# More weight tiles converted ahead of the second batch's folds, and more products behind those folds

## The chip, the cores and the metric

The kernel runs on one core of a Trainium2 chip. The metric is the device time of one execution in microseconds (us). The tensor engine is PE, its weight loads PEld, the vector engine DVE, the scalar engine ACT, GpSimd POOL, and SyncE, which here only issues transfers, SP. "L650" is line 650 of the kernel's file.

## The reference, cut to what matters

```python
# 4 batches, 8 heads, 768 rows, 64 wide; blocks of 64 rows: attention with decay
out[:, :, sl] = intra + inter                    # -> x of (4, 768, 512)
mixed = np.real(fft(fft(x, axis=1), axis=2))     # mix over rows, then over columns
u  = x + mixed
un = (u - mean(u)) / sqrt(var(u) + 1e-6)
ch = maximum(un @ w_ch1, 0) @ w_ch2              # 512x2048 and 2048x512, given as f64
return u + ch
```

## The kernel before: the parts that matter

A front (attention, folds of the rows, spectral products, norm) makes the rows of one batch after another. Beside it run the products with the weights of four groups of rows, the plain tiles (L636 with w1, L650 with w2); they fill PE while a front waits for DVE. The other eight groups, the late tiles, come last, as pairs with fewer products, and need linear combinations of the weights and of their own operands.

The weights arrive as f64 words and are converted on DVE and ACT, 32 tiles by one generator `w`. The front's generator yields a weight after each step, and the schedule puts so many units of products behind that step:

```python
            run(fold_a(b))
            yield 6.0 if b - 1 in LEADS else 3.0      # LEADS = (0,), so b = 1 here
            run(fold_b(b, sets))
            yield 12.0 if b - 1 in LEADS else 9.0     # L508
```

```python
    run(beside(mix, 24.0, beside(att1, 2.75 * t_chunk, w, 0.16 * NW), 0.16 * NW + 1.75 * t_chunk))
    half = [[mlp(b, g, h * FO // 2, (h + 1) * FO // 2) for b, g in PLAIN[:3]] for h in range(2)]
    ...
    t_rest, t_back = 3 * t_front - 5 * t_chunk, len(PLAIN) * t_mlp - 50.0   # 50.0: kept for the end
    ...
    run(weave(fr, back, (t_back - t_half) / (t_rest - t_rest * t_half / t_back)))
    front_end.close()
    ...
    load_u(0, nc.scalar)
    run(weave(combine_weights(0), back, 1.5))
    run(back)
    plain_end.close()
    psums.close()
    ...                                      # pools of the late tiles; p2: accumulators, 8 banks
    run(combine_weights(1))
    for j in range(len(LATE) // 2):
        late(j)
```

The boundary between the plain and the late tiles: what DVE does there.

```python
    def combine_weights(part):               # 16 pieces of 128x1024 on DVE, at L700
        if part == 0:
            todo = [(ws[:, 0], a21, a22, ADD), ...  # 3 sums of w1 -> w1s, 6 pieces
                    (wz[:, 0], b12, b11, SUB), ...] # 3 sums of w2 -> w2s, 6 pieces
        else:
            todo = [(a21, a11, a21, SUB), (b12, b22, b12, SUB)]   # in place, 4 pieces
        for o, x, y, op in todo:
            ...
                V.tensor_tensor(o[:, i:i + n // 2], x[:, i:i + n // 2], y[:, i:i + n // 2], op=op)
                yield 1.3

    # end of a plain tile (mlp), L660 to L663: ps is the accumulator of L650
                y = new(up, [128, DM], "y", bufs=1)
                tt(y[:, 0:HM], ps[:, 0:HM], u[:, 0:HM], op=ALU.add)                    # L661
                tt(y[:, HM:DM], ps[:, HM:DM], u[:, DM - 1:HM - 1:-1], op=ALU.add)      # L662
                store(b, T, y)               # L623: nc.sync.dma_start(...)

    def late(j):
        V.tensor_tensor(t[:, 0], b12, b11, op=SUB)       # L713 to L716: combinations "us"
        ...
            X, Y, Z = bank(), bank(), bank()
            prod(X, "a11", "b11", i, True)               # L723, needs no combination
            prod(Y, "a12", "b21", i, True)               # L723, needs none either
            prod(X, "s2", "t2", i, False)                # L723, needs w1s and us
```

## Time and profile before

| | before |
|---|---|
| time, median of 3 (range) | 823.18 us (821.59 to 825.39) |
| profiled span | 819.4 us |
| start to the first product with w1 | 96.2 us |
| first product with w1 to the first late product (L723): "the middle" | 331.9 us, PE idle 6.5 |
| first late product to the last addition on DVE (L799): "the late stage" | 388.2 us, PE idle 0.5 |

The last three rows are read off the lists of instructions in order of time; the 3.1 us by which their sum falls short of the span lie behind the last addition, where its result is stored. The profile's own lines are in the prediction below.

### The profile page before, as it was taken

To read this page: it belongs to the slowest core of one execution; us is meant where nothing else is said; L and a number is where in the kernel's file an instruction comes from. 1 tells how busy PE (TensorE), PEld (TensorE's weight loads), DVE (VectorE), ACT (ScalarE), POOL (GpSimd) and SP (SyncE) were. 2 spreads that over 40 slices of the span, in tenths; PEclk is the share of its full clock that TensorE was granted. 3 is DMA by queue.
4 is the path that set the end of the run, shared out by engine and by line. 5 is a ranking of instruction groups with operands and counts; after the bars stand their busy time and mean duration, and the time that the engine had idled before them with its cause. 6 is when DMAs were issued, how large, how long until landed. Compare 5 with 4: busy or idle time off the path is not lost.

```text
span 819.4 us, 11694 instructions
## 1 busy us (share of the span) xinstructions
PE 795.2 (97%) x4608; PEld 634.9 (77%) x4608; DVE 437.8 (53%) x1018; ACT 186.5 (23%) x448; POOL 86.1 (11%) x102
## 2 busy tenths in 40 slices
PE   6989899999999999999999999999999999999998
PEld 5777767768585857768648888888888888888886
DVE  5899798766743761354895541165313661146311
ACT  3756344225420211312002200022001210022100
POOL 3223340011011010220000000000000000000000
PEclk9999999999999999999999999999999999999999
DMA  9979624248741136530351011100111001010010
GB/s 233 249 154 271 174 90 129 63 113 201 203 125 51 52 62 131 129 123 26 93 162 42 1 53 51 52 1 1 64 40 52 0 1 39 33 33 0 1 39 26
DMA packets 126684, 68.88 MB, mean 84 GB/s; under 512 B 111150, under 2 KB 112174, under 8 KB 126630
## 3 DMA queue, kind: packets, MB, share of 16 engines
q1 hardware_dynamic: 121488, 55.67, 26.6%
q0 software_dynamic: 2112, 6.69, 2.4%
q10 hardware_dynamic: 3030, 5.78, 1.9%
q8 instruction: 36, 0.59, 0.3%
q14 instruction: 18, 0.15, 0.1%
HBM read 48.72 MB, written 19.40 MB: 83 GB/s over the span
## 4 chain that ended last, share of the span: by engine, by line
PE 80%; DVE 10%; issue 4%; DMA 3%; ACT 2%; POOL 1%; POOLq 0%; ACTq 0%; DVEq 0%
PE p L770 24%; PE p L723 24%; PE pm L650 10%; PE pm L636 8%; PE pa L332 3%; PE pa L516 3%; PE pa L298 3%; DMA x<-xb,ix 2%; PE pa L328 2%; PE pa L274 1%; DVE sc L302 1%; PE pa L315 1%; PE pa L348 1%; PE pa L279 1%; DVE stt L546 1%
## 5 line engine op out<-in xcount | busy, mean ns | idle before, releaser
L636 PE MATMUL pm<-ut,w 128*128 128x256 f32 x512 | 119.2, 382 | 0.0
L650 PE MATMUL pm<-w,hr 128*128 128x512 f32 x256 | 115.8, 597 | 0.2 <-DVE w L225 0.2
L636 PEld LDWEIGHTS pm<-ut,w 128*128 128x128 f32 x512 | 94.4, 190 | 15.4 <-issue 3.6
L723 PE MATMUL p<-ur,w 128*128 128x256 f32 x384 | 93.8, 379 | 0.0
L650 PEld LDWEIGHTS pm<-w,hr 128*128 128x128 f32 x256 | 46.6, 190 | 49.5 <-issue 48.0
L723 PEld LDWEIGHTS p<-ur,w 128*128 128x128 f32 x384 | 73.0, 190 | 10.3 <-issue 0.5
L723 PE MATMUL p<-us,w1s 128*128 128x256 f32 x256 | 65.7, 379 | 0.0
L770 PE MATMUL p<-w,hs 128*128 128x256 f32 x256 | 58.0, 379 | 0.5 <-DVE y L791 0.5
L770 PE MATMUL p<-w2s,hs 128*128 128x256 f32 x256 | 57.9, 379 | 0.0
L770 PE MATMUL p<-w,ha 128*128 128x256 f32 x256 | 57.9, 379 | 0.0
L770 PEld LDWEIGHTS p<-w,hs 128*128 128x128 f32 x256 | 48.5, 190 | 7.5 <-DVE y L791 0.9
L625 POOL DMA_INDIRECT out_dram<-y,ix x12 | 11.9, 989 | 402.6 <-DVE y L796 342.6
L770 PEld LDWEIGHTS p<-w2s,hs 128*128 128x128 f32 x256 | 48.6, 190 | 6.6
L723 PEld LDWEIGHTS p<-us,w1s 128*128 128x128 f32 x256 | 48.6, 190 | 6.6
L770 PEld LDWEIGHTS p<-w,ha 128*128 128x128 f32 x256 | 48.6, 190 | 6.6
L750 ACT COPY ha<-p 128x256 f32<-128x256 f32 x32 | 11.9, 372 | 169.1 <-PE p L723 139.4
L761 DVE TENSOR_TENSOR ha<-p,ha 128x256 f32<-128x256 f32 x32 | 13.6, 424 | 45.2 <-ACT ha L760 45.2
L298 PEld LDWEIGHTS pa<-qT,kT 64*128 64x128 f32 x384 | 26.0, 193 | 13.2 <-ACT qT L281 7.3
L302 DVE TENSOR_TENSOR sc<-pa,decay 128x512 f32<-128x512 f32 x48 | 31.5, 683 | 8.8 <-PE pa L298 8.5
L332 PE MATMUL pa<-sc,v 128*64 128x128 f32 x384 | 32.1, 284 | 4.1 <-DVE sc L302 4.1
L298 PE MATMUL pa<-qT,kT 64*128 64x128 f32 x384 | 30.7, 292 | 3.2 <-ACT qT L281 2.9
L270 POOL TENSOR_TENSOR kd<-k,decay 128x512 f32<-128x512 f32 x20 | 23.0, 1152 | 94.8 <-PE pa L315 64.5
(144 smaller groups left out, 1135.0 us busy)
## 6 DMA issues: line engine op xcount, KB each, us to landing
raw<-in_moe_w_ch_dram SPq DMA_DIRECT2D x32, 512.0 KB, 4.8
k<-in_k_dram SPq DMA_DIRECT2D x24, 256.0 KB, 5.0
q<-in_q_dram SPq DMA_DIRECT2D x24, 256.0 KB, 5.9
v<-in_v_dram SPq DMA_DIRECT2D x24, 256.0 KB, 4.9
ud<-x SPq DMA_DIRECT2D x16, 256.0 KB, 2.3
utd<-e SPq DMA_DIRECT2D x64, 64.0 KB, 2.2
u<-ud SPq DMA_DIRECT2D x16, 256.0 KB, 2.7
ur<-utd SPq DMA_DIRECT2D x6, 512.0 KB, 4.3
```

What stands on the lines that cost most here:

```text
L270: nc.gpsimd.tensor_tensor(kd, kt, kpow, op=ALU.mult)
L298: mm(pss[hi][:, hp, :], lhsT=kT[HD[hi], hp, :], rhs=qT[HD[hi], hp, :], start=True, stop=True)
L302: nc.vector.tensor_tensor(t, pss[hi], decay[:, hi::2, :], op=ALU.mult)
L328: mm(po[HD[hi], hp, :], lhsT=s_old[HD[hi], hp, :], rhs=qs[HD[hi], hp, :], start=(hp == 0), stop=False, skip_group_check=True)
L332: mm(po[HD[hi], hp, :], lhsT=vt[:, 2 * hp + hi, :], rhs=sc[hi][:, hp, :], start=(c == 0 and hp == 0), stop=(hp == HP - 1), skip_group_chec ...
L516: mm = nc.tensor.matmul(ps[0:m, n, :], lhsT=piece(a, i, n), rhs=cs[0:rows, a, i in (2, 3), n, :], start=(a == 0), stop=(a == 1))
L625: nc.gpsimd.indirect_dma_start(out=out.rearrange("b s d -> (b s) d"), out_offset=row_of(2 + HC * (b + 1) + T - HC), in_=y[:, :], in_offset ...
L636: nc.tensor.matmul(ps, lhsT=w1[:, c, 128 * fc:128 * fc + 128], rhs=ut[:, c, :], start=(c == 0), stop=(c == KO - 1))
L650: nc.tensor.matmul(ps, lhsT=hr[(fc - f0) // 4][:, fc % 4, 128 * i:128 * i + 128], rhs=w2[:, fc, :], start=(fc == f0), stop=(fc == f1 - 1))
L723: nc.tensor.matmul(ps, lhsT=s2.A[a][:, kt, 128 * i:128 * i + 128], rhs=U[b][:, kt, :], start=(first and kt == 0), stop=(kt == 1), skip_gro ...
L761: V.tensor_tensor(a22, two(Z), a22, op=ADD)
L770: nc.tensor.matmul(ps, lhsT=h[a][:, s, i, :], rhs=s2.B[b][:, i, :], start=(first and i == 0), stop=(i == HF - 1), skip_group_check=True)
```

## The change

Its intent: the weight tiles that the first products need are converted before the second batch's folds occupy DVE, and more products are kept for the time of those folds, so that PE has work while DVE folds.

```diff
             run(fold_b(b, sets))
-            yield 12.0 if b - 1 in LEADS else 9.0
+            yield 18.0 if b - 1 in LEADS else 9.0
@@
     run(beside(mix, 24.0, beside(att1, 2.75 * t_chunk, w, 0.16 * NW), 0.16 * NW + 1.75 * t_chunk))
+    run(part(w, 3.0))
     half = [[mlp(b, g, h * FO // 2, (h + 1) * FO // 2) for b, g in PLAIN[:3]] for h in range(2)]
```

## The prediction

> **What bounds the kernel now.** I read the page's busy times first, then a table of stages, then the tensor engine's waits inside the stages that the change touches, then the lists of instructions in order of time on the vector and scalar engines.
>
> ```profile
> PE 795.2 (97%) x4608; PEld 634.9 (77%) x4608; DVE 437.8 (53%) x1018; ACT 186.5 (23%) x448; POOL 86.1 (11%) x102
> ```
>
> The tensor engine (PE) is busy for 795.2 of 819.4 us, so all waits of the whole run together are 24.2 us. The stages, as busy time of each engine in five stretches:
>
> ```profile
> 0.00:94.00 94.00, 80.37 (x914) 65.29 (x914) 80.17 (x167) 52.26 (x115) 29.06 (x37) 1.00 0.87 214
> 94.00:132.00 38.00, 36.08 (x158) 25.10 (x159) 33.16 (x84) 14.18 (x35) 12.06 (x9) 1.00 0.41 129
> 132.00:245.00 113.00, 112.06 (x752) 81.31 (x751) 76.44 (x159) 42.43 (x92) 13.99 (x18) 1.00 0.54 141
> 245.00:428.00 183.00, 179.34 (x996) 123.06 (x995) 104.61 (x222) 29.59 (x80) 22.24 (x30) 1.00 0.35 89
> 428.00:819.00 391.00, 387.34 (x1793) 340.18 (x1791) 143.38 (x391) 48.06 (x128) 8.76 (x9) 1.00 0.09 30
> ```
>
> Columns are the stretch, its length, then busy PE, weight load, vector (DVE), scalar (ACT), GpSimd (POOL), clock, DMA share, GB/s. The reader is to see that PE is the bound from 94 us on: it idles 1.92, 0.94 and 3.66 us in the three middle stretches, 6.5 us together. The first 94 us run before anything that the change moves, and the last 391 us are products of the late tiles that it does not touch. So only those 6.5 us can be won. Who caused them, from the waits of PE between 92 and 428 us (longest last in each line):
>
> ```profile
> PE pa L569 <- DVE un L564: 3.1, 4, 1.0
> PE pa L516 <- DVE fe L475: 2.1, 3, 1.0
> PE pa L332 <- DVE sc L302: 1.8, 2, 1.6
> PE pm L650 <- DVE w L225: 0.2, 1, 0.2
> ```
>
> The wait that the change is aimed at is the last one: a product with w2 (L650) that waits for the eighth w2 tile to be converted (L225). It is 0.2 us. The other waits are for normalised rows (L564), for folds (L475) and for scores (L302). In time, the place looks like this on the vector engine (start, duration, and in brackets the idle time before and who ended it):
>
> ```profile
> 113.20 0.73 DVE L564 TENSOR_SCALAR un<-x,mv,rs 128x256 f32<-128x256 f32 x2 [0.93 <-POOL rs L551]
> ...
> 118.32 0.68 DVE L426 TENSOR_TENSOR fe<-x,x 128x512 f32<-128x512 f32 x1
> ...
> 123.48 0.69 DVE L426 TENSOR_TENSOR fe<-x,x 65x512 f32<-65x512 f32 x1 [0.18 <-DMA x<-xb,ix]
> ...
> 128.66 0.68 DVE L225 SCALAR_TENSOR_TENSOR w<-w,e 128x512 f32<-128x512 f32 x1
> ```
>
> The second batch's folds run from 118.3 to 128.7, between them a few conversions, and the vector engine is full. PE meanwhile has products:
>
> ```profile
> 116.18 12.18 PE L650 MATMUL pm<-w,hr 128*128 128x512 f32 x28
> 128.20 1.03 PE L636 MATMUL pm<-ut,w 128*128 128x256 f32 x4
> 129.40 1.12 PE L650 MATMUL pm<-w,hr 128*128 128x512 f32 x2 [0.17 <-DVE w L225]
> 130.36 2.79 PE L516 MATMUL pa<-cs,fe 128*128 128x193 f32 x16
> ```
>
> The folds are hidden already: L516, the first product that needs them, starts right behind L650. One product with f32 is two records here, so 28 records are 14 products in 12.0 us (116.18 to the next start at 128.20), 0.86 us each; the same reading of "x32" on L636 elsewhere gives 0.43 us each.
>
> **What the Trainium skill says.** "Perfetto Trace Analysis", Identifying the Most-Contended Engine, warns that matmul busy share is a bad measure of headroom and tells to use weight-load busy share. The trace agrees that it hides something: in the last stretch weight load is 340.18 of 391 us (87%), in the middle ones 66 to 73%, with PE shown full in all. But the spacing of 0.43 and 0.86 us per product is the same in the middle as in the last stretch, so I count idle time only. "PSUM — Partial Sum Buffer", Engine vs sequencer instructions, says that scalar, vector and GpSimd queues are strict FIFO and that matmuls start and complete in program order. This is the base of the whole argument: work put earlier in a queue delays what stands behind it. The 0.17 us above agrees: products for later folds stood behind the one that waited. "VectorE: DVE Perf Modes", The perf-mode tier table, gives f32 tensor_tensor the slow tier and tensor_scalar a faster one; here a 128x512 f32 tensor_tensor takes 0.68 us and the tensor_scalar steps of the conversion 0.42.
>
> **The change part by part.** It adds and removes no arithmetic. First, three more weight tiles (of 16 in the first half) are put in front of the products and the second batch's folds. One tile costs the vector engine L217, L222, L220 at 0.34 us from start to start and L224, L225 at 0.60: 2.2 us; three are 6.7 us (rounded up for the first of the next tile). On ACT a tile is two passes, about 1.2 us. The listing of instruction order shows them behind the statistics of the first rows, at about 93 to 108 us. There the vector engine has idle holes in the kernel before: 0.53, 1.96, 1.17, 0.53 and 0.93 us. Walking the new order with the old durations, the first hole costs nothing, the rows' second transpose is reached at 102.9 instead of 101.2, the next norm at 115.6 instead of 113.2, the folds start at about 121.6 instead of 118.3 and end at about 132 instead of 128.7. So half of the 6.7 us fills holes and about 3.3 us delays the folds. PE gets four more L636 (1.7 us) in front of the first transposes, which about covers their delay: gap 1.2 instead of 1.04 us. In front of the next ones only one L650 was moved: gap 1.6 plus 0.4 instead of 0.64. Plus 1.5 us so far.
>
> Second, the weight 12 to 18 sets more products before the first L516: in the new order 16 L650 and 8 L636 stand there, instead of 15 L650 and 2 L636. L516 is then reached at about 134, and the folds it needs end at about 130: no wait, and the 0.17 us are gone. The spectral products and the norms behind them come some 6.5 us later, with the products done earlier instead; the gap of 0.94 us at 146.7 has 8 L636 and 4 L650 (6.9 us) over it instead of 11 L636 (4.8 us) and should go. Minus 1.1 us.
>
> Third, a new wait: right after the L650s the new order has two groups of L636 for the next rows. The second needs the PSUM buffer that ACT frees (L644), and on ACT that stands behind a conversion step (L218) which needs the vector engine's L217, which stands behind the delayed folds, ending at 132. I work out 134.0 for the freeing, against 132.0 when PE gets there: plus 2.0 us.
>
> Fourth, later stages only shift. The third batch's folds have the same chain (product, L662, gather, fold) with as much work over it; 0.9 and 0.2 us stay. The 1.59 us at 292.8 has more products over its norms (16 L636 and 8 L650 instead of 19 L636) but fewer right before it; I take off 1.1. The 0.96 at 371.4 stays near 1.2.
>
> The sum: +0.2 +1.4 -0.2 -0.9 +2.0 -1.1 +0.2 = +1.6 us on gaps, so about 824.5; the terms are each uncertain by about 1 us. As two of the three losses hang on my estimate of when the folds end, I go a little back towards the old median: 824.0.
>
> **The rivals.** (a) The change does what it is meant to: waits of PE vanish and nothing comes in their place. For it: the vector engine's holes and the PSUM wait could be milder than I think. It cannot win more than 6.5 us, more likely 2: 821. (b) The vector engine becomes the bound at 94 to 132 us, as it is busy 33.16 of 38 us there already. Putting all 6.7 us on the path, with PE running dry, gives 828 to 830. Against it: PE has three tiles of half products ready, 27.6 us each (32 L636 and 16 L650), and only its fixed order can starve it. (c) Raw weights arrive late, as the raw tiles share buffers with the hidden rows, and block the vector and scalar queues. A raw tile lands 4.8 us after its issue (median), and 17.7 us of ACT's idle time before the sign step are put down to this already. It would lengthen the third point by 1 to 3 us: 825 to 827. (d) Everything is hidden and only PE's sum counts: 823.2 as before.
>
> **Range and chances.** All of them lie within 0.9% of 823.18; the three runs before spread from 821.59 to 825.39. Range 821.0 to 827.0. Faster than 806.7 would need more than every idle microsecond there is; slower than 839.6 would need 16 us of new waits.
>
> **What would show it.** Right: PE's idle time before 94 us and after 428 unchanged; no wait of L650 for L225; the folds of the second batch ending about 3 us later; the gap at 146.7 gone; a new gap near 132 with L636 waiting for ACT; transposes L569 waiting more near 113 to 118. Wrong: if the folds end no later, points one and three fall and the time is 821 to 822; if the gaps behind 245 us grow by several us, I misread the later stages.

## The result, and the profile after

The changed kernel took 831.27 us (828.35 to 832.07, 4 runs) against 823.2 us for the kernel before beside it: a ratio of 1.0096, 95% interval 1.0068 to 1.0124. It is slower, though within 2%, and outside the predicted 821 to 827. Ratios here are the mean time of one kernel's fast runs over that of the other's of the same rounds, so not quite the ratio of the quoted medians.

The table of stages of the changed kernel answers to that of the kernel before in the prediction (same columns; the last row is longer by the longer span):

```profile
0.00:94.00 94.00, 79.32 (x894) 64.97 (x894) 79.39 (x161) 51.89 (x114) 26.35 (x36) 0.98 0.89 225
94.00:132.00 38.00, 36.03 (x168) 24.53 (x167) 35.94 (x90) 16.19 (x37) 13.81 (x10) 1.00 0.43 129
132.00:245.00 113.00, 109.90 (x725) 80.05 (x724) 69.48 (x151) 39.08 (x86) 11.55 (x15) 1.00 0.48 120
245.00:428.00 183.00, 179.75 (x1028) 124.31 (x1028) 100.98 (x220) 30.71 (x83) 25.20 (x33) 1.00 0.35 88
428.00:830.00 402.00, 393.05 (x1799) 343.37 (x1797) 150.79 (x400) 47.99 (x128) 8.76 (x9) 0.99 0.10 33
```

The work is the same. What stands out is the last row: PE idles 8.95 us there in place of 3.66, and its busy time has grown by 5.7 us, part of it plain products that now lie behind 428 us, at a granted clock of 0.99. This is the stage that the change was said not to touch. The stages by PE's list:

| | before | after | after, run again (e8) |
|---|---|---|---|
| start to first product with w1 | 96.2 | 98.9 | 96.0 |
| the middle (PE idle in it) | 331.9 (6.5) | 331.8 (7.6) | 332.4 (6.8) |
| the late stage (PE idle in it) | 388.2 (0.5) | 396.6 (5.7) | 395.1 (5.7) |
| span | 819.4 | 830.3 | 826.5 |

The 2.7 us at the start are an accident of the profiled run: when the same kernel was run again, its start was that of the kernel before. The loss is in the late stage. PE's list at the boundary, first of the kernel before and then of the changed one (start, duration, records, and in brackets the idle time before and who ended it):

```profile
428.13 1.89 PE L723 MATMUL p<-ur,w 128*128 128x256 f32 x8
429.86 1.03 PE L723 MATMUL p<-us,w1s 128*128 128x256 f32 x4
```

```profile
430.63 1.03 PE L723 MATMUL p<-ur,w 128*128 128x256 f32 x4
436.84 2.05 PE L723 MATMUL p<-ur,w 128*128 128x256 f32 x4 [5.18 <-DVE y L662]
```

Before, the late products begin without a pause. After, four records run, then PE waits 5.18 us for L662, the last addition of the last plain tile, and the next four records take 2.05 us in place of 1.03. The clock over the boundary of the changed kernel, in two stretches of 12 us:

```profile
430.00:442.00 12.00, 6.82 (x18) 4.98 (x17) 7.38 (x12) 0.74 (x2) 1.08 (x1) 0.75 0.83 263
442.00:454.00 12.00, 12.00 (x55) 10.45 (x55) 6.33 (x19) 2.72 (x8) 0.00 (x0) 0.96 0.01 1
```

The third figure from the end is the granted clock: 0.75, then 0.96. The clock record of the trace has one stretch of 6.83 us at half speed here, from 436.05 to 442.88. "TensorE: Matmul & The Clock Gate", What's actually happening, in the Trainium skill describes a free-running window of 3413 ns after which an idle PE is halved. The trace agrees: the half-speed stretches behind this wait are 3413 ns long in e8, 6827 here and 13653 in e7. The run e8 has one window at the boundary and shows the sum cleanly: PE waits 5.15 us, and the eight records behind the wait take 3.31 us in place of 1.73, 1.6 us more (the window's start still lay in the wait). That makes 6.7 us, and its late stage is 395.08 - 388.18 = 6.90 us longer. In the first profiled run 16 records take 6.51 us in place of 3.45, so 5.18 and 3.1 make 8.2 against 8.4.

Why was DVE late? Its list at the boundary, before and after:

```profile
421.42 4.62 DVE L700 TENSOR_TENSOR w<-w 128x1024 f32<-128x1024 f32 x4
...
427.88 0.68 DVE L715 TENSOR_TENSOR us<-ur,us 128x512 f32<-128x512 f32 x1
428.49 0.41 DVE L661 TENSOR_TENSOR y<-pm,x 128x256 f32<-128x256 f32 x1
428.82 0.41 DVE L662 TENSOR_TENSOR y<-pm,x 128x256 f32<-128x256 f32 x1
```

```profile
428.86 4.59 DVE L700 TENSOR_TENSOR w<-w 128x1024 f32<-128x1024 f32 x4
...
435.30 0.69 DVE L715 TENSOR_TENSOR us<-ur,us 128x512 f32<-128x512 f32 x1
435.93 0.42 DVE L661 TENSOR_TENSOR y<-pm,x 128x256 f32<-128x256 f32 x1
436.28 0.41 DVE L662 TENSOR_TENSOR y<-pm,x 128x256 f32<-128x256 f32 x1
```

In both, DVE is full from the last norm on: combinations of the weights, combinations of the late operands, last addition. Call the time from the last spectral products to that addition DVE's tail, and the time from the same products to PE's first late product the cover. Measured from the last spectral products (L532, the last of them at 395.18 and 401.13), L662 ends after 34.05 us before and 35.56 after. What changed is PE's side: it reaches the first late product 32.95 us after the last spectral products before, and 29.50 us after. The products of the plain tiles are a fixed number. The change takes more of them early, behind the second batch's folds, so fewer are left to cover DVE's tail: 3.45 us of cover are gone and the tail is 1.5 us longer (more steps of the last norms are left behind those products: the first combination starts 8.9 us after them before and 10.3 us after). Together that is 4.9 us. Before, the first combined operand that a late product needs (L714's, ready at 427.36) was there 2.5 us before its product at 429.86. A loss of 4.9 us against 2.5 us of slack gives a wait of 2.4 us; run e2 below has just that, and the changed kernel has more, because it waits for L662 already.

### The profile page after: what moved, and what is told of

Read it like the earlier page. It is cut to its first block, busy times and chain, and to the rows that moved or that the text cites.

```text
span 830.3 us, 11700 instructions
## 1 busy us (share of the span) xinstructions
PE 798.0 (96%) x4608; PEld 637.2 (77%) x4608; DVE 436.6 (53%) x1018; ACT 185.9 (22%) x448; POOL 85.7 (10%) x102
## 4 chain that ended last, share of the span: by engine, by line
PE 77%; DVE 12%; DMA 5%; issue 3%; ACT 1%; POOL 1%; SPq 0%; DVEq 0%; ACTq 0%; POOLq 0%
PE p L723 24%; PE p L770 23%; PE pm L636 8%; PE pm L650 7%; PE pa L332 3%; PE pa L298 3%; PE pa L516 3%; DMA x<-xb,ix 2%; PE pa L328 2%; PE pa L274 1%; PE pa L348 1%; PE pa L315 1%; PE pa L279 1%; DVE w L224 1%; DMA raw<-in_moe_w_ch_dram 1%
## 5 line engine op out<-in xcount | busy, mean ns | idle before, releaser
L650 PE MATMUL pm<-w,hr 128*128 128x512 f32 x256 | 115.7, 596 | 0.0
L723 PE MATMUL p<-ur,w 128*128 128x256 f32 x384 | 95.9, 385 | 5.2 <-DVE y L662 5.2
L723 PEld LDWEIGHTS p<-ur,w 128*128 128x128 f32 x384 | 74.0, 193 | 16.2 <-issue 6.0
L650 PEld LDWEIGHTS pm<-w,hr 128*128 128x128 f32 x256 | 46.7, 190 | 48.5 <-issue 47.1
L723 PE MATMUL p<-us,w1s 128*128 128x256 f32 x256 | 67.0, 385 | 0.0
L723 PEld LDWEIGHTS p<-us,w1s 128*128 128x128 f32 x256 | 49.7, 194 | 7.1
L723 PE MATMUL p<-us,w 128*128 128x256 f32 x128 | 32.8, 379 | 0.0
```

Of the source, the lines that this page charges most:

```text
L650: nc.tensor.matmul(ps, lhsT=hr[(fc - f0) // 4][:, fc % 4, 128 * i:128 * i + 128], rhs=w2[:, fc, :], start=(fc == f0), stop=(fc == f1 - 1))
L723: nc.tensor.matmul(ps, lhsT=s2.A[a][:, kt, 128 * i:128 * i + 128], rhs=U[b][:, kt, :], start=(first and kt == 0), stop=(kt == 1), skip_gro ...
```

## The experiments

All ran beside the kernel before, each on one chip, and all gave correct results. Theory A: the loss is the boundary, where too few products cover DVE's tail. Rival B: the conversions ahead of the folds delay the folds, and that is the loss. Rival C: the wait hangs on something else at the boundary.

### The two halves of the change, and the cover by itself: e1 to e4

e1 is the changed kernel with the weight back at 12 (conversions alone), e2 the kernel before with 18 (weight alone), e3 the kernel before with less kept for the end, e4 the changed kernel with more kept:

```diff
-            yield 18.0 if b - 1 in LEADS else 9.0        # e1: in the changed kernel
+            yield 12.0 if b - 1 in LEADS else 9.0
-            yield 12.0 if b - 1 in LEADS else 9.0        # e2: in the kernel before
+            yield 18.0 if b - 1 in LEADS else 9.0
-    t_rest, t_back = 3 * t_front - 5 * t_chunk, len(PLAIN) * t_mlp - 50.0
+    t_rest, t_back = 3 * t_front - 5 * t_chunk, len(PLAIN) * t_mlp - 44.0   # e3, in the kernel before
+    t_rest, t_back = 3 * t_front - 5 * t_chunk, len(PLAIN) * t_mlp - 56.0   # e4, in the changed kernel
```

> First part of the change alone: three weight tiles converted before the second batch's folds, the weight behind the folds left at 12. Theory A (the loss is made at the seam at 428 to 437 us, where too few products are left behind the last spectral products to cover the vector engine's combining of the weights): the order leaves 32.7 us of products there, as the kernel before has, so L723 waits under 0.5 us for L662, the clock stays full at the seam, and the time is 823 to 827, with one wait of 2 to 3 us of L516 near 129 us. Rival B (the 6.7 us of conversions in front of the folds are the loss): within 1.5 us of the changed kernel, about 831.

> Second part alone: the weight behind the folds 18, the conversions where they were. Theory A: the order leaves 29.2 us of products behind the last spectral products, as the changed kernel does, so L723 waits 3.5 to 5.5 us at the seam and the clock is halved for 6.8 us behind it; 829 to 832. Rival B: as the kernel before, 822 to 825, without a wait at the seam.

> Neither part of the change; only the reserve of products for the end of the front is cut from 50 to 44 in the kernel before, which leaves 27.5 us of products behind the last spectral products instead of 32.7. Theory A: the same wait of 4 to 7 us at the seam and a halved clock behind it, 830 to 834, although no fold and no conversion of the second batch has moved. Rival B: 822 to 825.

> Both parts of the change, and the reserve raised from 50 to 56, which leaves 34.4 us of products behind the last spectral products. Theory A: the wait at the seam and the halved clock behind it go, 8.5 us less than the changed kernel: 821 to 824. Rival B: as the changed kernel, 829 to 832.

| | time (ratio to before, interval) | cover: last spectral to first late product | wait at the boundary | middle |
|---|---|---|---|---|
| before | 822.4 | 32.95 | none | 331.9 |
| e1 conversions alone | 820.64 (0.9983, 0.9966 to 1.0) | 32.95 | none | 330.9 |
| e2 weight alone | 824.67 (1.0024, 1.0005 to 1.0044) | 29.50 | 2.40 | 329.8 |
| e3 before, 6 units less kept | 824.73 (1.0036, 1.0019 to 1.0052) | 27.77 | 2.35 | 330.8 |
| e4 after, 6 units more kept | 824.33 (1.0032, 1.0003 to 1.006) | 35.22 | none | 333.0 |

e2's boundary, on PE:

```profile
427.67 1.89 PE L723 MATMUL p<-ur,w 128*128 128x256 f32 x8
431.96 2.04 PE L723 MATMUL p<-us,w1s 128*128 128x256 f32 x4 [2.40 <-DVE us L714]
```

B falls: with the conversions alone there is no loss and no wait, and the wait of L516 that was expected of e1 did not appear. The wait goes with the cover, not with the conversions: it is in e2 and in e3, which has neither part of the change, and it is gone in e4. The sizes were off: e2 and e3 wait 2.4 us, half of what was expected, and their times lie 4.3 and 5.3 us under the expected ranges; e2's four records after it are slowed to 2.04 us. (e3 has less cover than e2 and the same wait, as its tail is shorter too: 33.73 against 35.51 us.) Eight records run first there, and PE then waits for L714's combination, not for L662. The programs that the kernels compile to suggest why: the accumulators lie in eight banks; that of the last plain tile is in bank 7 in the changed kernel and in bank 6 in e2, and in both the second group of late products gets bank 7 and the fourth bank 6. So in the changed kernel the second group must wait until L662 has read that bank. On this reading 2.4 of its 5.15 us come from the lost cover, as in e2, and the rest from where that accumulator happened to lie.

e4 is not a pure cure: its late stage is back at 388.2 us, but its middle is 1.3 us longer than in the changed kernel's profile and two of its four runs have a clock of 0.996 (826.3 and 826.5 us, the others 822.0 and 822.3). Why the middle is longer is left open.

### The bank: e5 and e9, which moved nothing

```diff
+        if j == 0:
+            bank(), bank()                         # e5
-            X, Y, Z = bank(), bank(), bank()
+            X, Z, Y = bank(), bank(), bank()       # e9
```

> The changed kernel with one edit: two unused accumulator tiles are taken at the start of the late tiles, so that their first product groups fall two banks further and no longer on the bank that the last addition of the plain tiles reads. Theory A (DVE's tail after the last folds ends too late) with the bank as a part of it: eight first records run before the wait instead of four, the wait names L715's operand (us) instead of L662's y, falls from 5.18 us to 3 to 4.5, and the second stretch of half clock may shorten: 827 to 831. If the bank has nothing to do with it: the same wait of about 5.2 after four records, 829 to 832.

> The last test of the bank had an edit that moved nothing (the allocator goes by what is free, not by a ring). Here the changed kernel takes its accumulators for each late group in the order X, Z, Y, so that the compiled program gives the bank of the last plain tile to the fourth product group (Z) and a free one to the second (Y). Bank as a part of the cause: eight first records run before the wait; it names L715's us and is 3.3 to 3.6 us instead of 5.15; the span behind the first late product falls by 0.8 to 1 us from 395.1 to 396.6: 826 to 830. Bank without a part: wait of 5.2 after four records.

e5 took 828.57 us (1.0065, 1.0043 to 1.0086) and e9 829.07 (1.0083, 1.0067 to 1.0098), with waits of 5.14 and 5.13 after four records. This is no verdict on the bank: the compiled programs have the accumulators at the boundary in the same banks and the same order as the changed kernel, because banks are given out by what is free, not by the order of the names. They serve as repeats.

### The repeats: e8 (changed kernel) and e6 (conversions alone)

> The changed kernel again, unedited, with five rounds on this chip, for the half-clock stretch of 3.4 us that the profiled run showed at 23 to 26 us, where its instructions are those of the kernel before. If it belongs to the change: nearly all runs have a mean granted clock near 0.994, and the time is 830 to 832. If it is chance at the start: a good part of the runs have 0.996 and lie near 828.4, and the median is 828 to 831. In either case slower than the kernel before by 0.6 to 1.1 per cent.

> A repeat, with five rounds, of the version with the early conversions alone (weight 12 kept), because its first result (820.6 against 822.4, interval touching 1.0) was at the edge. Theory A: no wait at the first products of the late tiles, 819.5 to 822, again a little under the kernel before. Rival B (the conversions delay the folds and that is the loss): slower than the kernel before, over 824.

e8 took 827.99 us (827.23 to 831.28), ratio 1.0065 (1.0044 to 1.0087). With e5 and e9, whose order and banks at the boundary are the same, the ratios are 1.0065 to 1.0096 in four measurements. The dip of the clock at the start of the first profile does not belong to the change: e8's profile has none there, and five of its six runs have a clock of 0.996 or 0.998, where the first profile had 0.994. e8 has its second window at 133.8 us, behind the new wait near 132 (the third term under "Why the prediction was wrong"): eight records take 3.56 us there, where the first profile has 1.99. e6 took 820.85 us, ratio 0.9978 (0.9961 to 0.9995), again without a wait: the conversions alone are a gain of 0.2 per cent, just clear of the noise.

### Shortening DVE's tail: e7 and e10, which left or worsened the wait

e7 gives the last four pieces of the combinations to GpSimd. e10 moves the eight w2 pieces into the first late pair in program order:

```diff
-                V.tensor_tensor(o[:, i:i + n // 2], ...)
+                (nc.gpsimd if part else V).tensor_tensor(o[:, i:i + n // 2], ...)     # e7
```

```diff
             last = (i, X, Z)
+            if j == 0:                             # e10; part 2: wz's six pieces and b12's two
+                next(s2.w2_later, None)
```

> The changed kernel with one edit: the second part of the weight combinations (four pieces of 128x1024, 4.6 us of DVE, right ahead of the combinations of the late tiles) goes to GpSimd. PE's order is untouched. Theory A: DVE's tail behind the last spectral products shrinks by 4.6 us, from 34.9 to about 30.2 us, against 29.5 us of products; the wait of 5.18 us falls to under 1 us, no half clock there, and the span behind the first late product returns from 396.6 to 388 to 389.5: 820.5 to 824.5. Rival C (the wait comes from the bank or from something else than DVE's load): the wait stays above 4 us and the time at 829 to 832.

> The changed kernel, with the eight w2 pieces of the weight combinations (9.3 us of DVE) moved from in front of the late tiles into the first late pair, one behind each group of its products, where DVE is idle most of the time; their results are needed only by the products with w2, some 50 us on. PE's order is the same, and GpSimd is left alone. Theory A: DVE's tail behind the last spectral products falls from 34.9 to about 25.5 us, below the 29.5 us of products, so the wait of 5.15 us and the half clock behind it go, and the span behind the first late product is 388.2 to 389.5: 819 to 823, that is no longer slower than before. Rival (the loss lies elsewhere, in the early conversions or the longer weights): 827 and more.

e7 took 835.79 us (1.0157), its wait 12.64 us. It is no test of A, as it brought its own loss. DVE's list while GpSimd works:

```profile
422.60 3.01 DVE L700 TENSOR_TENSOR w2s<-w 128x1024 f32<-128x1024 f32 x1
425.54 2.76 DVE L564 TENSOR_SCALAR un<-x,mv,rs 128x256 f32<-128x256 f32 x2
```

These take 1.18 and 0.72 us in the changed kernel. "SBUF — State Buffer", SBUF: two separate sides, says that DVE with two SBUF inputs, or in a two-port mode, and GpSimd lock a shared pair of ports for a whole instruction; 1.8 and 2.0 us of delay beside GpSimd pieces of 2.34 us fit that. On top, L661 sat idle for 4.35 us until a store from y had landed.

e10 took 830.73 us (1.0118, 1.01 to 1.0136): A had expected 819 to 823. DVE's list (the edit shifts lines by three: L703 is L700, L718 is L715):

```profile
423.18 0.70 DVE L718 TENSOR_TENSOR us<-ur,us 128x512 f32<-128x512 f32 x1
...
430.05 2.37 DVE L703 TENSOR_TENSOR w<-w 128x1024 f32<-128x1024 f32 x2
432.32 0.43 DVE L661 TENSOR_TENSOR y<-pm,x 128x256 f32<-128x256 f32 x1
```

The late operands were ready at 423.88, 3.3 us before the first late product, and still PE waited 5.03 us for L662. So the combined operands are not what PE waits for. The scheduler had put all eight pieces, which are free to run early, in front of the last addition, which must wait for PE. The queue goes in order, so the addition ended at 433.09, 35.41 us after the last spectral products, as before the edit. A must be sharpened: what counts is the place of the last addition in DVE's queue.

e11 and e12 make e10's edit in e2's kernel (weight alone) and in the kernel before:

> The kernel before with the weight 18 alone and the same move of the w2 pieces. Theory A: the middle keeps its gain of 2 us (329.8 in place of 331.9) and the wait of 2.4 us at the late products goes: 818.5 to 822, perhaps the fastest of all. Rival: no gain over the 824.7 of the weight alone.

> The control: the kernel before with the same move of the w2 pieces. There DVE's tail (33.4 us to its last needed result) was already just inside the products' 32.95 plus the first records' 1.9, so theory A expects no gain here: 820.5 to 824, ratio 0.997 to 1.002. If the move is worth 5 us of its own wherever it is made, 816 to 819, and run e10 would prove nothing about the change.

e11 took 824.27 us (1.0028, 1.0016 to 1.004) and waited 2.55 us, most likely for the same addition: the profile names no releaser, but L662 ended at 434.09, 0.10 us before the wait did. PE's waits at the boundary, first in e10, then in e11:

```profile
433.23 2.05 PE L726 MATMUL p<-ur,w 128*128 128x256 f32 x4 [5.03 <-DVE y L662]
```

```profile
430.51 1.13 PE L726 MATMUL p<-us,w1s 128*128 128x256 f32 x4 [0.42 <-ACT ha L753]
434.19 2.02 PE L726 MATMUL p<-ur,w 128*128 128x256 f32 x4 [2.55 <-issue]
```

e10's wait comes after four records, at the second group, and e11's after twelve, at the fourth. These are the groups with the bank of the last plain accumulator, and neither needs a combined operand, so this speaks for the bank. e12, the control, took 822.24 us (1.0005, 0.9993 to 1.0017): where the cover suffices the move is worth nothing.

### Taking both holders away: e13 to e18

e13 lays w2s over the plain tiles' x buffers, so that its pieces can't start before the last addition has read x. e14 and e15 do the same in e2's kernel and in the kernel before:

```diff
-            wz = s2.wz = s2.wp.tile([128, 3, HF, HM], F32, name="w2s")
+    s2.wz = ctx.enter_context(tc.tile_pool(name="wz", bufs=1, side="right",
+                              reuse_waits="tile")).tile([128, 3, HF, HM], F32, name="w2s")
     s2.hp = ctx.enter_context(tc.tile_pool(name="h2", bufs=1, side="right", reuse_waits="tile"))
```

> The changed kernel, the w2 pieces moved into the late tiles as before, and their result tile (w2s) now placed over the plain tiles' x buffers, so that the pieces can't start before the last addition of the plain tiles (L662) has read x: the compiled order of DVE has them behind L662. PE's order is the same. Sharpened theory A: L662 ends about 1 us after the last product of the plain tiles instead of 6, the wait of 5.0 to 5.2 us falls below 0.6 us, no half clock at the boundary, and the span from the first late product to the last is 388.2 to 389.5: 819.5 to 823. If something else at the boundary makes the wait, or the loss lies in the earlier stages: 826 and more.

> The kernel before with the weight 18 alone and the same move. Sharpened theory A: the wait of 2.4 to 2.6 us falls below 0.6 us, the middle stays at 329.5 to 330, so 817.5 to 821.5, up to 0.4 per cent under the kernel before. Otherwise the 824.3 of the earlier runs stays.

> The control: the kernel before with the same move. It has no wait there, so by theory A nothing is gained: 820.5 to 824, ratio 0.997 to 1.003. If the move itself were worth several us, 817 or less.

e13 took 828.1 us (1.009, 1.0075 to 1.0106): the wait fell to 3.21 us only. Its last addition, on DVE, and the store that it waited for, in SP's queue:

```profile
430.63 0.42 DVE L661 TENSOR_TENSOR y<-pm,x 128x256 f32<-128x256 f32 x1 [7.02 <-DMA out_dram<-y]
```

```profile
418.73 7.49 SPq L581 DMA_DIRECT2D utd<-e  x8
426.26 1.10 SPq L587 DMA_DIRECT2D ud<-x  x2
427.46 0.40 SPq L623 DMA_DIRECT2D out_dram<-y  x1
```

With the pieces gone DVE sat idle for 7.02 us: the addition overwrites the only buffer y, whose content from the tile before, ready at 416.94, was still to be stored. SP issued that store at 427.46, behind eight stores of the late tiles' rows (L581), the last of which wait for DVE's transposes. In e14 the wait at the boundary fell to 1.32 us, again at the fourth group. But e14 (826.87, 1.0072) and e15 (824.14, 1.0039) got slower than without the edit. PE waited in both later in the first late pair for an addition behind the moved pieces (L763 there; 3.20 and 1.75 us). That is a cost of this way of moving them.

e16 adds one more edit to e13, the store of that tile issued by ACT; e17 has that edit alone; e18 is e16's pair of edits in e2's kernel:

```diff
-                store(b, T, y)
+                store(b, T, y, queue=nc.scalar if (b, g) == PLAIN[3] else nc.sync)
```

> The changed kernel with the w2 pieces behind the last plain addition, and in addition the store of the last plain group's first tile issued by ScalarE instead of SyncE, so that the buffer y comes free without waiting for the late tiles' stores. The scheduler now also puts eight product groups that need no combined operand first. If the two together are the cause: L662 ends within 1.3 us of the last plain product, the wait is under 0.6 us, clocks are near 1.0 and the time is 819.5 to 823.5. If the boundary still waits 2 us or more, a third cause is there: 826 and more.

> The changed kernel with that store alone moved to ScalarE's queue, one line; the w2 pieces stay in front of the last plain addition in DVE's queue, but the late tiles' own combinations now stand behind it (2.8 us). If DVE's queue is the main holder: L662 ends about 2.8 us earlier relative to the last spectral products (32.6 to 33 us in place of 35.5), the wait falls from 5.15 to 2 to 2.8 us, and the time is 824 to 828. If the store were the main holder, the wait would be gone here as well: 819.5 to 823.5.

> The kernel before with the weight 18 alone, the w2 pieces behind the last plain addition and the last plain store on ScalarE's queue. If the boundary was all that the weight cost: no wait over 0.6 us there, the middle 329.5 to 330.5, the time 818 to 821.5, ratio 0.995 to 0.999. If the weight costs elsewhere too: 822 and more.

e17, the store alone, took 827.96 us (1.0065, 1.0047 to 1.0084), at the upper end of its expected time; its wait is 2.61 us, as A had it. DVE's queue:

```profile
426.31 4.59 DVE L700 TENSOR_TENSOR w<-w 128x1024 f32<-128x1024 f32 x4
430.81 0.42 DVE L661 TENSOR_TENSOR y<-pm,x 128x256 f32<-128x256 f32 x1
```

L661 starts with no idle time, right behind weight pieces. e16, with both, took 822.79 us (0.9999, 0.9976 to 1.0022). PE at the boundary, and the last addition on DVE:

```profile
431.59 7.38 PE L725 MATMUL p<-ur,w 128*128 128x256 f32 x32
```

```profile
431.79 0.42 DVE L661 TENSOR_TENSOR y<-pm,x 128x256 f32<-128x256 f32 x1 [3.90 <-PE pm L650]
```

L725 is L723 here. The addition now waits for PE's own product and nothing else, and the 5.15 us have become 0.08. The late stage is 388.5 us against 388.2 before. The scheduler changed the order of the first late products in e16, e17 and e18 as well: eight groups that need no combined operand come first. In e16 this is not what removed the wait: the combined operands were ready at 427.27, 4.3 us before the first late product, and its second group, again on bank 7, waited 0.08 us. In e17, where they were ready only at 434.09, the order may have helped. e16's runs split: three at a clock of 0.999 or 1.0 take 820.5 to 822.0, three with more time at half clock (0.994 to 0.997) 823.6 to 825.5; the profiled one, of the latter, has windows at 27 and 136 us and none at the boundary.

e18 took 820.56 us (0.9979, 0.995 to 1.0007), with no wait at the boundary (0 where e2 had 2.4) and a middle of 330.4: level with the conversions alone, and not told apart from the kernel before.

## Why the prediction was wrong

- **What failed: "the last 391 us are products of the late tiles that it does not touch"**, and with it "Fourth, later stages only shift". It is true of the instructions and false of the wait. The first late products stand behind DVE's tail, and the change took 3.45 us of the products that covered it. I had the number: the prediction says that products are done "earlier instead", but the sum never asked where they would then be missing. Its own sign, "PE's idle time ... after 428 unchanged", is the one that failed: 0.5 us became 5.7. Worth +6.9 us in the clean repeat, 5.15 of wait and 1.6 of half clock.
- **The first term, +1.5 us on transposes** (gaps of 1.2, and 1.6 plus 0.4, against 1.04 and 0.64), was mis-sized: measured 0.94 and 0.34 us, so a gain of 0.4. The conversions cost PE nothing there. e1 and e6 show them to be worth 0.8 to 1.0 us in the middle.
- **The second term** was partly right. L650's wait for L225 is gone. The gap of 0.94 us is not: two gaps of 0.36 and 0.56 us came in its place at 160 to 162 us.
- **The third term, a new wait of 2.0 us near 132**, was right. PE's list of the changed kernel:

```profile
132.30 1.89 PE L636 MATMUL pm<-ut,w 128*128 128x256 f32 x8
136.34 1.99 PE L636 MATMUL pm<-ut,w 128*128 128x256 f32 x8 [2.15 <-ACT hr L644]
```

  It is 2.1 to 2.3 us in every full-change kernel with the 50.0 kept, and in neither e1 nor e2: only the two parts together make it. That is most of why their gains in the middle (1.0 and 2.1 us) vanish when joined. In e5, e8, e9 and e16 a half-clock window follows it as well, which the prediction did not count (1.6 us in e8). The cause given was right as well: the folds end 2.5 us later in e8 (131.28 against 128.75), where about 3 was said.
- **The sum for the middle** was near by luck: +1.6 us of idle time predicted, +1.2 measured in the first profile and +0.4 in the repeat, but the first term was 1.9 us too high and the second 0.9 too low. The middle as a whole got hardly longer (331.9, then 331.8 and 332.4). The gap of 1.59 us at 292.8 closed wholly (I took off 1.1), 0.68 us came up at 362.4. (The weight load of the middle stretches is 66 to 72% by the prediction's own table, not 66 to 73; nothing rests on it.)
- **Rivals**: (b), DVE as the bound at 94 to 132 us, named a loss of the right size (828 to 830) in the wrong place. DVE was the bound at the boundary, and no rival looked there.

What is shown: the wait is held by the place of the last plain addition in DVE's queue and by the store ahead of its buffer in SP's queue; taking away one leaves 3.2 or 2.6 us, taking both leaves 0.08. What is only argued: the bank as the reason why the changed kernel waits after four records and e2 after eight. It is read from the compiled programs, and the place of the wait in e10, e11 and e14 fits it, but both edits meant to test it moved no bank.

## What to carry to other kernels

Where a fixed stock of work covers waits, spending it in one place takes it from another: before moving products forward, count what is left in front of the next boundary and set it against the busy engine's tail there. "Not touched" has to be checked on the releasers of a stage's first instruction, not on its own code. And moving work in program order is not moving it in the queue: look at the compiled order before reading a result.

## What the Trainium skill lacked or had wrong

- "TensorE: Matmul & The Clock Gate", HAM oscillation — how this bites in real kernels: its rule is to have no PE-idle gaps over some 3.4 us. Here e2's gap of 2.40 us was followed by records at half speed (2.04 us for four instead of 1.03), and e17's of 2.61 us by a stretch of 3413 ns at half clock; e14 had gaps of 1.32 and 3.20 us without one. Shorter gaps can cost a window too, by where they fall: e14's 3.20 us lay half in each of two windows, e2's 2.40 almost wholly in one. Counting PE's idle time in every such window of the 20 profiles up to 800 us, all 15 at full speed with 1.8 us or more of it were followed by one at half speed, none with under 1.2 us was, and between the two some were.
- "PSUM — Partial Sum Buffer", Engine vs sequencer instructions: it names the scalar, vector and GpSimd queues as strict FIFO and leaves out SyncE, which issues transfers. In e13 a store whose data was ready at 416.94 us was issued at 427.46, behind stores whose data was not.
- No page that I read has the point on cover: how many microseconds of products must stand in front of a boundary, measured as 29.5 us against a DVE tail of 35.6.
